# Moving the row statistics, the weight scans and some loads of a fused attention-and-GLU kernel

## The chip, the core and the metric

The kernel runs on one core of one Trainium2 chip. Time is device microseconds (us) of one execution from its first to its last instruction, with what lies around it; less is better. A profile gives the span of one execution and the times of every instruction within it. The engines are PE (matmuls), PEld (its weight loads), DVE (VectorE), ACT (ScalarE), POOL (GpSimd) and SP (SyncE, which here only issues DMAs).

## The reference

```python
x = A_x                                   # 2048 rows of 640, bf16
xn = layernorm(x)
q = xn @ wq                               # 32 heads of 192
p = softmax(q @ k_last512.T * 192**-0.5)  # each head has its own 512 keys and values
s = (p @ v_last512) @ wo
h = sigmoid(xn @ w_gate) * (xn @ w_up)    # 1536 wide
g = silu(h @ w_down)
out = x + s * g
```

## The kernel before, in words

The kernel has three stages. **Stage B** (lines 275 to 581, about the first 150 us) normalizes the rows and makes `h`. It goes over four groups `s` of 512 rows and in each over `NF` = 12 blocks `f` of 128 hidden columns (lines 474 and 479). A block is ten matmuls of 512 columns, five on the gate weights and five on the up weights (line 486), into one of four pairs of PSUM banks in turn; then ACT takes the sigmoid (line 491) and DVE multiplies into `hT_sb` (line 492). For the groups 0 to 2, `h` is stored to DRAM (`h_d`, line 554); for the last one the product with `w_down` follows at once (line 560).

**The rows of the next group** are made ready inside the blocks of this one. `load_x4` loads 512 rows in one DMA. `ln_at[s]` names the block at which the statistics begin (`ln_stats`, DVE), how many row tiles each block takes, and the block at which ACT takes the square root (`ln_rstd`). After that `ln_rest` does two row tiles in each of two blocks: `ln_apply` (DVE, line 372) writes the normalized tile `xn`, from a pool with three buffers, and SP issues a DMA transpose into `xnT` (line 441). A matmul of the next group reads all four transposed tiles. `xnT[1]` and `xnT[3]` are one buffer, `x_odd`; `xnT[0]` and `xnT[2]` lie in the big tile `mid`. In the odd groups `swap` copies halves of `x_odd` with four DMAs, and `sum_x` adds them up on DVE, for the faster matrix product of the next stage.

**Scans.** The weights are scaled by powers of two before they are added up in fp16, so an upper bound of each weight's size is wanted first. `wq` comes in 16 pieces of 480 KB into seven buffers (`scan_load`); a piece is taken by ACT (`scan_abs`, line 301: a sum of absolute values) or by DVE (`scan_fold`, lines 207 and 209: a running maximum). `abs_hw` does the same for the up weights (four pieces) and the down weights (four). The first seven `wq` pieces are loaded from SP's queue and nine from POOL's, each when the piece before it in its buffer is done. `set_scale` reduces the results, sends them through DRAM to all partitions (two POOL DMAs, lines 213 and 214), and `set_scale2` makes the scale. After that `load_raw` brings `wq` in pieces of 2 x 192 KB on 64 partitions each (POOL, line 230), and ACT and DVE scale and add them up (`scale_w`, `sum_w`). `load_k`, `scale_k` and `turn_k` load a pair of heads' keys, scale them (DVE, line 167) and transpose them with a DMA (line 172).

**Attention** (to about 680 us) has 16 runs, `r`: scores and exponentials in 16 steps `k` (`stage_s`), then eight products with the values (`stage_pv`), while `phase_s` and the loop around it issue what later runs want. **The last stage** (line 1103 on) multiplies by `wo` (steps `O`) and, for the groups 0 to 2, by `w_down` (steps `D`), with a seven-product scheme on half matrices; its extra operands are made by DVE (`scale_down`, `sum_down`). A step `D` leaves its gate rows in one of three buffers (`gate_rows`), from which POOL stores them to `gB_d` (line 1052).

Every engine and every queue takes its instructions in the order of the program; the program's order is written out by hand in the tables `sums`, `folds`, `abs_in`, `abs_at`, `ln_at` and in the conditions on `(s, f)` and `(r, k)`. An engine runs ahead of the others as far as its own waits allow, so a DMA issue that waits for nothing goes out long before the block under which it is written.

Of the kernel before, what the change touches and what calls it, by code (L numbers as in the profile page):

```python
# [8 lines left out]
AF = mybir.ActivationFunctionType  # L9
# [8 lines left out]
def kernel(  # L18
# [13 lines left out]
    nc = tc.nc  # L32
# [242 lines left out]
    with ExitStack() as bctx:  # L275
# [17 lines left out]

        wmax = bone.tile([P, NCD, NSC], BF16, name="wmax")
        mx_row = bone.tile([P, P], F32, name="mx_row")
        scans = bone.tile([P, 13], F32, name="scans")
# [6 lines left out]
        def abs_hw(n):  # L303
            v = wu_sb[:, :, 3 * n * P:3 * (n + 1) * P] if n < 4 else wd_sb[:, 3 * (n - 4):3 * (n - 3), :]
            nc.scalar.activation(
                scan_out.rearrange("p (c n) -> p c n", c=v.shape[1]), v, AF.Abs, accum_out=hw_sum[:, n:n + 1])

        def load_x(t):
            x_sb = xin_pool.tile([P, D], BF16, name=f"x_sb{t}")
            nc.sync.dma_start(x_sb[:], xf[t * P:(t + 1) * P, :])  # L310
            x_tiles[t] = x_sb[:]

        def load_x4(s):
            x_sb = xin_pool.tile([P, TQ, D], BF16, name="x_sb4")
            nc.sync.dma_start(
                x_sb[:], xf[s * 512:(s + 1) * 512, :].rearrange("(q p) d -> p q d", p=P)
            )
            for q in range(TQ):
                x_tiles[s * TQ + q] = x_sb[:, q, :]
# [131 lines left out]
        def sum_x(pi, k, x_sw):  # L451
# [12 lines left out]
            elif k == 5:  # L464
                tt(xb[HI], ev[HI], xb[HI], ALU.subtract)

        sums = {(1, 6): (0, 4), (2, 0): (0, 0), (2, 1): (0, 1), (2, 9): (0, 2), (2, 10): (0, 3), (2, 11): (0, 5),
                (3, 2): (1, 0), (3, 4): (1, 1), (3, 7): (1, 2)}
        folds = {(1, 0): 5, (1, 1): 6, (1, 9): 13, (1, 10): 14}
        abs_in = [(0, 6), (0, 7), (0, 9), (0, 10), (0, 11), (1, 1), (1, 2), (1, 4), (1, 5), (1, 7), (1, 8), (1, 10)]  # L470
        scan_act = dict(zip(abs_in, [i for i in range(NPC) if i not in folds.values()]))
        abs_at = [(2, 1), (2, 2), (2, 4), (2, 5), (2, 9), (2, 10), (3, 4), (3, 10)]
        ln_at = {0: (5, (1, 1, 2), 8), 1: (2, (1, 1, 1, 1), 6), 2: (2, (1, 1, 1, 1), 6)}
        for s in range(NST):
            hT_sb = hpool.tile([P, TQ, NF, P], BF16, name="hT_sb")
            pi = s // 2
# [2 lines left out]
            for f in range(NF):  # L479
# [31 lines left out]
                if (s, f) in folds or (s, f) in scan_act:  # L511
                    done = []
                    if (s, f) in folds:
                        done.append(folds[s, f])
                        scan_fold(wmax, done[-1], s == 1 and f == 0)
                    if (s, f) in scan_act:
                        done.append(scan_act[s, f])
                        scan_abs(done[-1], 1 + abs_in.index((s, f)))
                    for i in sorted(done):
                        if i + NSB < NPC:  # L520
                            scan_load(i + NSB, nc.gpsimd)
                if (s, f) in abs_at:
                    abs_hw(abs_at.index((s, f)))
                if s == 1 and f == NF - 1:
                    nc.vector.tensor_reduce(
                        scans[:, 0:1], wmax[:].rearrange("p c n -> p (c n)"), axis=mybir.AxisListType.X, op=ALU.max)
# [3 lines left out]
                elif s == 2 and f == 0:  # L530
                    set_scale(scans[:], mx_row)
                elif s == 2 and f == 1:
                    nc.sync.dma_start(wd_sb[:], B_w_down.rearrange("(f p) d -> p f d", p=P))
                if s == 2 and 2 <= f < 5:
                    load_raw(0, f - 2, nc.gpsimd)
                elif s == 2 and f == NF - 1:
                    set_scale2(mx_row)
                elif s == 3:
                    for c in {0: (0,), 2: (1,), 5: (2,), 8: (3,)}.get(f, ()):
                        scale_w(0, c)  # L540
                    for c in {1: (0,), 3: (1,), 6: (2,), 9: (3,)}.get(f, ()):
                        sum_w(0, c)
                        load_raw((c + 3) // NCD, (c + 3) % NCD, nc.gpsimd)
                    if f in (0, 6):
                        scale_k((0, f // 6))
                    elif f in (3, 9):
                        turn_k((0, f // 6))
                    if f == 2:
                        load_k((0, 1), nc.gpsimd)
            if s + 2 < NST:  # L550
                load_x4(s + 2)
# [203 lines left out]
    def load_wo(n):  # L755
        nc.sync.dma_start(wo_in[n % 4], wo_r[:, n * NWC:(n + 1) * NWC, :])
# [40 lines left out]
    steps = [(k[0], int(k[1:])) for k in "O0 O1 D0 D1 O2 D2 D3 O3 D4 D5 O4 O5 O6 O7".split()]  # L797
    steps += [("O", m) for m in range(8, 16)]
    wd_r = B_w_down.rearrange("(f p) d -> p f d", p=P)

    def tiles_of(j):
        kind, m = steps[j]
# [47 lines left out]
    def phase_s(r, pi, g, k, q_list, pv_list):  # L850
# [24 lines left out]
        if r in (2, 4) and k == 7:  # L875
            set_scale(*((hw_sum[:, 0:4], mx_rows[0], mx_h, 3) if r == 2 else (hw_sum[:, 4:8], mx_rows[0], mx_w, 4)))
        if r in (3, 5) and k == 0:
            set_scale2(mx_rows[0], *((mx_h, h_up, h_down, 0.25) if r == 3 else (mx_w, wd_up, wd_down)))
        if r == 6 and k == 0:
# [33 lines left out]
    for r, (pi, g) in enumerate(runs):  # L913
# [51 lines left out]
    NOD = NH * DN  # L965
    down_raw = [part(arm, n * NOD, (NH, DN), F16) for n in range(4)]
    T0, T1 = (free[n].rearrange("p a b -> p (a b)") for n in range(2))
    down_sum = [t.rearrange("p (a b) -> p a b", b=DN) for t in (T0[:, 0:NOD], T0[:, NOD:2 * NOD], T1[:, 0:NOD])]
    down_ops = [down_raw[0], down_sum[0], down_sum[1], down_raw[1], down_raw[2], down_raw[3], down_sum[2]]
# [45 lines left out]

    def keep(b, dst):
        nc.scalar.activation(dst, ps_all[:, b, 0:DN], AF.Copy)  # L1017

    def load_down(n, k, d):
        nc.sync.dma_start(down_ops[n].bitcast(BF16), wd_r[:, k * NH:(k + 1) * NH, d])  # L1020
# [84 lines left out]
    for j in range(NP):  # L1105
# [20 lines left out]
                product(j + 1, 4 - X, "A11", 0, True)  # L1126
                keep(4 - X, p1s[:])

        if j == 0:
            for part_ in (0, 0, LEFT), (4, 0, RIGHT), (5, 1, RIGHT), (3, 1, LEFT):  # L1130
                load_down(*part_)
        if j + 2 < NP:
            load_quads(j + 2)
        side(j, 0)
# [74 lines left out]
```

## Time and profile before

| | us |
|---|---|
| median of 3 runs (905.4 to 909.42) | 905.8 |
| the profiled execution | 908.94 |
| its span, from the first to the last instruction | 906.8 |
| PE busy in the span | 874.4 |
| idle PE between matmuls in stage B, groups 0 to 3 and the product with `w_down`, gaps over 0.5 us after the first 10 us | 18.45 |
| idle PE between matmuls in the last stage, gaps over 0.1 us | 4.81 |

A line of the waits names who waited, for whom, and then the total in us, the number of times and the longest. A line of the timeline has start and length in us, engine, line, operation, tiles and count; in brackets the engine's idle time before it and what ended it. A line of the table by stretches has for each engine the busy time and the count of instructions, then the clock granted to PE, the mean share of the 16 DMA engines, and GB/s. In the chain of waits a piece is start, length and who held the end.

### The profile page before, as it was taken

The numbers are of one execution on the slowest core, as the hardware profiler recorded it, in microseconds if no ns is written. First come the engines' busy times: TensorE is split into PE (matmuls) and PEld (weight loads), VectorE is DVE, ScalarE is ACT, GpSimd is POOL, SyncE is SP. The second block draws the span as 40 slices with busy tenths as digits, with TensorE's granted clock in tenths as the row PEclk, the third lists the DMA queues.
The fourth block names the chain that finished last, engine by engine and source line by source line (L and its number), as shares of the span: only waits on it lengthen the run. The fifth ranks groups of instructions, "written<-read, shape, count | busy, mean of one in ns | idle before, by whom it ended". The sixth has DMA issues, their size and how long they took to land.

```text
span 906.8 us, 18988 instructions
## 1 busy us (share of the span) xinstructions
PE 874.4 (96%) x7569; PEld 569.5 (63%) x7569; DVE 675.5 (74%) x1134; ACT 624.1 (69%) x770; POOL 235.1 (26%) x330
## 2 busy tenths in 40 slices
PE   9799798999999999999999999899998999999998
PEld 5244244576577577567667657657676776777775
DVE  4468565777687687776777777588886687888997
ACT  4687367648877968968968878664665665666662
POOL 0131124822443344245236226400000111000000
PEclk9899899999999999999999999999999999999999
DMA  9997892275999996897798799599889797466751
GB/s 269 297 265 202 177 134 88 60 170 148 214 135 206 205 227 118 210 217 116 216 228 121 203 186 145 139 261 219 198 164 247 225 300 262 147 211 220 261 178 38
DMA packets 255385, 172.90 MB, mean 191 GB/s; under 512 B 159584, under 2 KB 238688, under 8 KB 255296
## 3 DMA queue, kind: packets, MB, share of 16 engines
q1 hardware_dynamic: 246624, 144.31, 63.6%
q0 software_dynamic: 8672, 27.37, 14.6%
q8 instruction: 59, 0.97, 0.5%
q14 instruction: 30, 0.25, 0.1%
HBM read 100.47 MB, written 35.13 MB: 150 GB/s over the span
## 4 chain that ended last, share of the span: by engine, by line
PE 83%; DMA 7%; issue 3%; DVE 3%; ACT 2%; SPq 0%; POOL 0%; DVEq 0%; POOLq 0%; ACTq 0%
PE ps_all L606 20%; PE ps_all L714 19%; PE ps_all L1010 19%; PE ps_all L700 18%; PE ps_all L486 6%; DMA kraw<-in_A_k_cache_dram 3%; DMA x_odd<-xn 2%; PE ps_all L560 1%; DMA gB_d<-op 1%; DVE hT_sb L492 1%; PE ps_all L395 1%; DMA arm<-in_B_w_down_dram 1%; DMA x_sb<-in_A_x_dram 0%; ACT mid L301 0%; ACT sig_sb L491 0%
## 5 line engine op out<-in xcount | busy, mean ns | idle before, releaser
L704 ACT ACTIVATE E<-ps_all 128x1024 bf16<-128x1024 f32 x256 | 251.1, 1021 | 124.8 <-PE ps_all L700 124.2
L700 PE MATMUL ps_all<-qT,kT 64*128 64x512 bf16 x1536 | 198.1, 376 | 0.0
L714 PE MATMUL ps_all<-v_sb,E 128*128 128x193 bf16 x2048 | 175.8, 248 | 2.3 <-DVE qT L644 2.3
L714 PEld LDWEIGHTS <-E 128*128 128x128 bf16 x2048 | 171.1, 98 | 10.8 <-issue 10.6
L644 DVE TENSOR_TENSOR qT<-ps_all,qp 128x512 bf16<-128x512 f32 x174 | 115.5, 687 | 48.5 <-PE ps_all L606 38.2
L1010 PEld LDWEIGHTS <-mid 128*128 128x128 f16 x1176 | 115.0, 98 | 49.9 <-issue 5.4
L700 PEld LDWEIGHTS <-kT 64*128 64x128 bf16 x1536 | 84.9, 94 | 79.4 <-issue 4.4
L627 DVE COPY qp<-ps_all 128x512 f32<-128x512 f32 x150 | 100.5, 686 | 45.9 <-PE ps_all L606 45.9
L721 DVE TENSOR_TENSOR o_st<-ps_all,rden 128x768 bf16<-128x768 f32 x128 | 122.5, 957 | 4.6 <-DVE rden L720 0.2
L606 PE MATMUL ps_all<-mid 64*128 64x512 f16 (+1 forms) x840 | 106.4, 376 | 0.4 <-DVE qT L644 0.4
L606 PE MATMUL ps_all<-mid,arm 64*128 64x512 f16 (+1 forms) x840 | 105.6, 376 | 0.0
L606 PEld LDWEIGHTS <-mid 64*128 64x128 f16 x840 | 49.0, 94 | 44.1 <-issue 2.1
L606 PEld LDWEIGHTS <-arm 64*128 64x128 f16 x840 | 47.2, 94 | 44.7 <-issue 0.5
L1010 PE MATMUL ps_all<-arm,mid 128*128 128x320 f16 x462 | 67.5, 299 | 2.0 <-ACT p1s L1017 2.0
L830 ACT ACTIVATE mid<-mid,w_sc 128x1536 f16<-128x1536 bf16 (+1 forms) x41 | 60.2, 1493 | 0.0
L244 ACT ACTIVATE mid<-mid,w_sc 128x1536 f16<-128x1536 bf16 x37 | 58.2, 1572 | 2.7 <-DVE w_sc L222 1.7
L230 POOL DMA_DIRECT2D mid<-in_A_wq_dram x80 | 48.2, 607 | 43.9 <-DVE mid L266 43.0
L492 DVE TENSOR_TENSOR hT_sb<-ps_all,sig_sb 128x512 bf16<-128x512 f32 x48 | 32.6, 684 | 32.9 <-ACT sig_sb L491 17.0
L1010 PE MATMUL ps_all<-op,mid 128*128 128x320 f16 x378 | 55.1, 299 | 0.0
L1010 PE MATMUL ps_all<-mid 128*128 128x320 f16 x336 | 48.4, 299 | 2.8 <-DVE acc L1059 2.6
L491 ACT ACTIVATE sig_sb<-ps_all 128x512 bf16<-128x512 f32 x48 | 28.2, 594 | 31.8 <-PE ps_all L486 25.6
L486 PEld LDWEIGHTS <-wg_sb 128*128 128x128 bf16 x225 | 22.4, 101 | 43.3 <-issue 17.9
(187 smaller groups left out, 1073.0 us busy)
## 6 DMA issues: line engine op xcount, KB each, us to landing
oT_d<-oT SPq DMA_DIRECT2D x64, 384.0 KB, 5.8
mid<-oT_d SPq DMA_DIRECT2D x46, 384.0 KB, 5.3
mid<-in_A_wq_dram POOLq DMA_DIRECT2D x80, 192.0 KB, 6.4
arm<-in_A_wo_dram SPq DMA_DIRECT2D x16, 480.0 KB, 5.5
v_sb<-in_A_v_cache_dram SPq DMA_DIRECT2D x28, 192.0 KB, 5.7
kraw<-in_A_k_cache_dram SPq DMA_DIRECT2D x26, 192.0 KB, 4.5
h_d<-hT_sb SPq DMA_DIRECT2D x12, 384.0 KB, 3.8
mid<-in_A_wq_dram POOLq DMA_DIRECT2D x9, 480.0 KB, 7.5
```

What stands on the lines that cost most here:

```text
L230: eng.dma_start(raw[r], wq_r[:, c, :, g * GC:(g + 1) * GC])
L244: nc.scalar.activation(raw.bitcast(F16), raw, AF.Copy, scale=w_up)
L486: nc.tensor.matmul(gu[:, i, :], lhsT=w[:, c, f * P:(f + 1) * P], rhs=xnT[s][:, c, :], start=(c == 0), stop=(c == NCD - 1),)
L606: nc.tensor.matmul(ps_all[:, b, :], lhsT=w(r, c), rhs=x[r, c, :], start=(first and k == 0), stop=(k == len(cs) - 1), skip_group_check=True,)
L627: nc.vector.tensor_copy(dst, part(b))
L644: nc.vector.tensor_tensor(q_out(i, u, pp), part(b), t, ALU.add)
L700: nc.tensor.matmul(ps[:, b, :], lhsT=kT[h, c * PC + j, :], rhs=qT_t[r][i, j][h, pp, :], start=(j == 0), stop=(j == PC - 1),)
L704: nc.scalar.activation(E_t[r, i, pp][:, c, :, :], ps, AF.Exp, scale=scale_qk)
L714: nc.tensor.matmul(o_ps[:, q // 2, q % 2, 0:DH + 1], lhsT=E[:, c, h, q * P:(q + 1) * P], rhs=vt[:, c, 0:DH + 1], start=(c == 0), stop=(c = ...
L721: nc.vector.tensor_tensor(o_st[:, :, h * DH:(h + 1) * DH].rearrange("p (b i) d -> p b i d", b=2), o_ps[:, :, :, 0:DH], rden[:].to_broadcas ...
L830: eng.activation(t, t.bitcast(BF16), AF.Copy, scale=up)
L1010: nc.tensor.matmul(ps_all[:, b, d0:d1], lhsT=a[:, c, :], rhs=w[:, c, d0:d1], start=(start and c == 0), stop=(c == nk - 1), skip_group_chec ...
```

## The change

- `ln_at`: the statistics of the next group begin at block 2, 1 and 0 (before 5, 2, 2) and the square root is taken at block 5, 5 and 4 (before 8, 6, 6). The transposes go out at blocks 5 and 6, 6 and 7, 5 and 6 (before 8 and 9, 7 and 8, 7 and 8). `xpool` has four buffers, not three.
- `load_x4(1)` stands among the weight loads, after the fourth of six; `load_x4(s + 2)` stands at block 8, not at the end of the group.
- SP loads four scan pieces at the start, three more (4, 5, 6) at block 8 of group 0, and pieces 9 and 10 after the stores of group 0. POOL loads the other seven. ACT takes 13 pieces, DVE three (11, 12, 14).
- The up weights are scanned at blocks 3 and 4 of group 0 and 8 and 10 of group 2. The down weights are no longer scanned in stage B: in the runs 1, 3, 5 and 7 SP loads a piece of them beside `wo`, and ACT scans it in the run after; their scale is made in runs 10 and 11 (before 4 and 5).
- The six loads of the first three `raws` stand at the end of group 1, ahead of the value and key loads (before: after the first `set_scale`, in blocks 2 to 4 of group 2). `set_scale` goes from block 0 of group 2 to block 2.
- The load of `wd_sb` goes from block 1 of group 2 to block 7. In group 3, `load_k((0, 1))` goes from block 2 to 0 and its `scale_k` from 6 to 7.
- The four loads of the down operands go from the start of the last stage to run 15, step 8; the `scale_down` calls go a little later in the first step. `gate_rows` has five rows.

```diff
-        xpool = bctx.enter_context(tc.tile_pool(name="xpool", bufs=3))
+        xpool = bctx.enter_context(tc.tile_pool(name="xpool", bufs=4))
...
             if k < 2:
                 load_x(2 + k)
+            elif k == 3:
+                load_x4(1)
...
-        load_x4(1)
-        for i in range(NSB):
+        for i in range(4):
             scan_load(i, nc.sync)
...
-        folds = {(1, 0): 5, (1, 1): 6, (1, 9): 13, (1, 10): 14}
...
+        folds = {(1, 7): 11, (1, 8): 12, (1, 9): 14}
+        scan_act = {(0, 7): 0, (0, 8): 1, (0, 9): 2, (0, 10): 3, (1, 1): 4, (1, 2): 7, (1, 3): 5, (1, 5): 8, (1, 6): 6,
+                    (1, 8): 9, (1, 9): 10, (2, 0): 13, (2, 1): 15}
+        abs_at = [(0, 3), (0, 4), (2, 8), (2, 10)]
+        ln_at = {0: (2, (1, 1, 2), 5), 1: (1, (1, 1, 1, 1), 5), 2: (0, (1, 1, 1, 1), 4)}
-        ln_at = {0: (5, (1, 1, 2), 8), 1: (2, (1, 1, 1, 1), 6), 2: (2, (1, 1, 1, 1), 6)}
...
+                    if i + NSB < NPC and i not in (2, 3):
+                        scan_load(i + NSB, nc.gpsimd)
...
+                if s + 2 < NST and f == 8:
+                    load_x4(s + 2)
+                    if s == 0:
+                        for i in (4, 5, 6):
+                            scan_load(i, nc.sync)
                 if s == 1 and f == NF - 1:
+                    for c in range(3):
+                        load_raw(0, c, nc.gpsimd)
                     for hp in range(G):
                         load_v(0, hp, nc.gpsimd)
                     load_k((0, 0), nc.gpsimd)
...
-                elif s == 2 and f == 1:
+                elif s == 2 and f == 7:
                     nc.sync.dma_start(wd_sb[:], B_w_down.rearrange("(f p) d -> p f d", p=P))
-                if s == 2 and 2 <= f < 5:
-                    load_raw(0, f - 2, nc.gpsimd)
...
-                    if f == 2:
+                    if f == 0:
                         load_k((0, 1), nc.gpsimd)
...
+                if s == 0:
+                    for i in (9, 10):
+                        scan_load(i, nc.sync)
...
+            if g < 4:
+                nc.sync.dma_start(wo_in[(3 * g + 3) % 4], wd_r[:, 3 * g:3 * g + 3, :])
...
+        if r == last and k == 8:
+            for part_ in (0, 0, LEFT), (4, 0, RIGHT), (5, 1, RIGHT), (3, 1, LEFT):
+                load_down(*part_)
...
+            if pi == 0 and 1 <= g < 5 and k == 6:
+                w = wo_in[3 * g % 4]
+                nc.scalar.activation(w, w, AF.Abs, accum_out=hw_sum[:, 3 + g:4 + g])
...
+    gate_rows += [end.tile([P, D], BF16, name=f"gate{n}")[:] for n in range(2)]
...
-    for n, p in zip((0, 4, 5, 3), (1, 3, 6, 7)):
+    for n, p in zip((0, 4, 5, 3), (3, 6, 7, 8)):
         at("O0", p, scale_down, n)
```

More of the change, by code (lines that the diff above doesn't have):

```diff
@@ L295 @@
         mx_row = bone.tile([P, P], F32, name="mx_row")
-        scans = bone.tile([P, 13], F32, name="scans")
+        scans = bone.tile([P, 14], F32, name="scans")
         scan_out = bone.tile([P, 3 * D], BF16, name="scan_out")
@@ L301, in scan_abs, with abs_up @@
             nc.scalar.activation(scan_t[i], scan_t[i], AF.Abs, accum_out=scans[:, col:col + 1])
-        def abs_hw(n):
-            v = wu_sb[:, :, 3 * n * P:3 * (n + 1) * P] if n < 4 else wd_sb[:, 3 * (n - 4):3 * (n - 3), :]
+        def abs_up(n):
             nc.scalar.activation(
-                scan_out.rearrange("p (c n) -> p c n", c=v.shape[1]), v, AF.Abs, accum_out=hw_sum[:, n:n + 1])
+                scan_out.rearrange("p (c n) -> p c n", c=NCD), wu_sb[:, :, 3 * n * P:3 * (n + 1) * P], AF.Abs,
+                accum_out=hw_sum[:, n:n + 1])
         def load_x(t):
@@ L465, in sum_x @@
                 tt(xb[HI], ev[HI], xb[HI], ALU.subtract)
-        sums = {(1, 6): (0, 4), (2, 0): (0, 0), (2, 1): (0, 1), (2, 9): (0, 2), (2, 10): (0, 3), (2, 11): (0, 5),
+        sums = {(1, 5): (0, 4), (1, 10): (0, 0), (1, 11): (0, 1), (2, 7): (0, 2), (2, 8): (0, 3), (2, 9): (0, 5),
                 (3, 2): (1, 0), (3, 4): (1, 1), (3, 7): (1, 2)}
-        folds = {(1, 0): 5, (1, 1): 6, (1, 9): 13, (1, 10): 14}
-        abs_in = [(0, 6), (0, 7), (0, 9), (0, 10), (0, 11), (1, 1), (1, 2), (1, 4), (1, 5), (1, 7), (1, 8), (1, 10)]
-        scan_act = dict(zip(abs_in, [i for i in range(NPC) if i not in folds.values()]))
-        abs_at = [(2, 1), (2, 2), (2, 4), (2, 5), (2, 9), (2, 10), (3, 4), (3, 10)]
-        ln_at = {0: (5, (1, 1, 2), 8), 1: (2, (1, 1, 1, 1), 6), 2: (2, (1, 1, 1, 1), 6)}
+        folds = {(1, 7): 11, (1, 8): 12, (1, 9): 14}
[3 more added lines that the diff above has]
+        ln_at = {0: (2, (1, 1, 2), 5), 1: (1, (1, 1, 1, 1), 5), 2: (0, (1, 1, 1, 1), 4)}
         for s in range(NST):
@@ L510 @@
                     sum_x(*sums[s, f], sw)
[L511 to L521, printed above, removed]
-                if (s, f) in abs_at:
-                    abs_hw(abs_at.index((s, f)))
+                for i, fold in ((folds.get((s, f)), True), (scan_act.get((s, f)), False)):
+                    if i is None:
+                        continue
+                    if fold:
+                        scan_fold(wmax, i, i == 11)
+                    else:
+                        scan_abs(i, 1 + list(scan_act).index((s, f)))
+                    if i + NSB < NPC and i not in (2, 3):
+                        scan_load(i + NSB, nc.gpsimd)
+                if (s, f) in abs_at:
+                    abs_up(abs_at.index((s, f)))
+                if s + 2 < NST and f == 8:
[3 more added lines that the diff above has]
+                            scan_load(i, nc.sync)
                 if s == 1 and f == NF - 1:
-                    nc.vector.tensor_reduce(
-                        scans[:, 0:1], wmax[:].rearrange("p c n -> p (c n)"), axis=mybir.AxisListType.X, op=ALU.max)
+                    for c in range(3):
+                        load_raw(0, c, nc.gpsimd)
                     for hp in range(G):
@@ L530 @@
                 elif s == 2 and f == 0:
+                    nc.vector.tensor_reduce(
+                        scans[:, 0:1], wmax[:].rearrange("p c n -> p (c n)"), axis=mybir.AxisListType.X, op=ALU.max)
+                elif s == 2 and f == 2:
                     set_scale(scans[:], mx_row)
-                elif s == 2 and f == 1:
+                elif s == 2 and f == 7:
                     nc.sync.dma_start(wd_sb[:], B_w_down.rearrange("(f p) d -> p f d", p=P))
-                if s == 2 and 2 <= f < 5:
-                    load_raw(0, f - 2, nc.gpsimd)
-                elif s == 2 and f == NF - 1:
+                if s == 2 and f == NF - 1:
                     set_scale2(mx_row)
@@ L543 @@
                         load_raw((c + 3) // NCD, (c + 3) % NCD, nc.gpsimd)
-                    if f in (0, 6):
-                        scale_k((0, f // 6))
+                    if f in (0, 7):
+                        scale_k((0, f // 7))
                     elif f in (3, 9):
-                        turn_k((0, f // 6))
-                    if f == 2:
+                        turn_k((0, f // 9))
+                    if f == 0:
                         load_k((0, 1), nc.gpsimd)
-            if s + 2 < NST:
-                load_x4(s + 2)
             if s < NM3:
@@ L799, with load_down @@
     wd_r = B_w_down.rearrange("(f p) d -> p f d", p=P)
+    NOD = NH * DN
+    down_raw = dict(zip((0, 3, 4, 5), (part(arm, n * NOD, (NH, DN), F16) for n in range(4))))
+    def load_down(n, k, d):
+        nc.sync.dma_start(down_raw[n].bitcast(BF16), wd_r[:, k * NH:(k + 1) * NH, d])
     def tiles_of(j):
@@ L874, in phase_s @@
             abs_v(g, (1, 3, 4, 5).index(k))
-        if r in (2, 4) and k == 7:
+        if r in (2, 10) and k == 7:
             set_scale(*((hw_sum[:, 0:4], mx_rows[0], mx_h, 3) if r == 2 else (hw_sum[:, 4:8], mx_rows[0], mx_w, 4)))
-        if r in (3, 5) and k == 0:
+        if r in (3, 11) and k == 0:
             set_scale2(mx_rows[0], *((mx_h, h_up, h_down, 0.25) if r == 3 else (mx_w, wd_up, wd_down)))
-        if r == 6 and k == 0:
+        if r == last and k == 1:
             nc.vector.tensor_tensor(g_scale, h_down, wd_down, ALU.mult)
+        if r == last and k == 8:
+            for part_ in (0, 0, LEFT), (4, 0, RIGHT), (5, 1, RIGHT), (3, 1, LEFT):
+                load_down(*part_)
         if r == last - 3 and k == 7:
@@ L964 @@
     ops[1] = [free[2]] + [part(arm, n * NO, (KB, DN), F16) for n in range(2)] + [free[3], free[4], free[1], free[0]]
-    NOD = NH * DN
-    down_raw = [part(arm, n * NOD, (NH, DN), F16) for n in range(4)]
     T0, T1 = (free[n].rearrange("p a b -> p (a b)") for n in range(2))
     down_sum = [t.rearrange("p (a b) -> p a b", b=DN) for t in (T0[:, 0:NOD], T0[:, NOD:2 * NOD], T1[:, 0:NOD])]
-    down_ops = [down_raw[0], down_sum[0], down_sum[1], down_raw[1], down_raw[2], down_raw[3], down_sum[2]]
+    down_ops = [down_raw[0], *down_sum[:2], *(down_raw[n] for n in (3, 4, 5)), down_sum[2]]
     gate_rows = [T1[:, NOD + n * D:NOD + (n + 1) * D].bitcast(BF16) for n in range(3)]
+    gate_rows += [end.tile([P, D], BF16, name=f"gate{n}")[:] for n in range(2)]
     down_tmps = [acc[order[n]][:, d] for n in (14, 15) for d in (LEFT, RIGHT)]
@@ L1017, in keep @@
         nc.scalar.activation(dst, ps_all[:, b, 0:DN], AF.Copy)
-    def load_down(n, k, d):
-        nc.sync.dma_start(down_ops[n].bitcast(BF16), wd_r[:, k * NH:(k + 1) * NH, d])
     def scale_down(n):
@@ L1127, in ahead @@
                 keep(4 - X, p1s[:])
-        if j == 0:
-            for part_ in (0, 0, LEFT), (4, 0, RIGHT), (5, 1, RIGHT), (3, 1, LEFT):
-                load_down(*part_)
         if j + 2 < NP:
```

## The prediction, made before the changed kernel ran

> **What bounds it now.** PE is busy for 874.4 of the 906.8 us of the span, so I read the waits of PE first:
>
> ```profile
> PE ps_all L486 <- DMA x_odd<-xn: 13.2, 2, 6.7
> PE ps_all L560 <- DVE hT_sb L492: 3.0, 3, 2.0
> PE ps_all L1010 <- DVE acc L1059: 2.6, 1, 2.6
> ...
> PE ps_all L1010 <- ACT p1s L1017: 2.0, 1, 2.0
> PE ps_all L486 <- DVE hT_sb L492: 1.4, 1, 1.4
> ...
> PE ps_all L486 <- DMA mid<-xn: 0.9, 1, 0.9
> ```
>
> Half of the waiting is for `x_odd`, the transposed rows of groups 1 and 3. The timeline of PE shows the place, and a second price:
>
> ```profile
> 33.95 1.24 PE L486 MATMUL ps_all<-mid,wu_sb 128*128 128x512 bf16 x5
> 41.91 2.29 PE L486 MATMUL ps_all<-x_odd,wg_sb 128*128 128x512 bf16 x5 [6.72 <-DMA x_odd<-xn]
> 44.00 2.34 PE L486 MATMUL ps_all<-x_odd,wu_sb 128*128 128x512 bf16 x5
> 46.13 1.83 PE L486 MATMUL ps_all<-x_odd,wg_sb 128*128 128x512 bf16 x5
> 47.80 1.24 PE L486 MATMUL ps_all<-x_odd,wu_sb 128*128 128x512 bf16 x5
> ...
> 104.02 2.29 PE L486 MATMUL ps_all<-x_odd,wg_sb 128*128 128x512 bf16 x5 [6.45 <-DMA x_odd<-xn]
> ```
>
> Five matmuls take 1.08 us from start to start (33.95 against 32.87). After 6.72 us of idleness the next three fives take 5.89 us (41.91 to 47.80), not 3.24: 2.65 us for the clock, which the stretch from 40 to 45 us gives as 0.55. Group 3 pays 6.45 and 2.32 in the same way (104.02 to 109.58). With 0.87 before group 2, 1.41 in group 3 and 0.54, 0.50 and 1.96 in the product with `w_down`, stage B loses 18.45 + 4.97 = 23.4 us. In the last stage 2.61, 2.04 and 0.16 are lost, 4.8 in all. That is about what there is to win, 28 us.
>
> Why are the transposes late? Partly because they are issued late (30.82 and 91.22 us), and because the fourth waits for a buffer of `xn` until the first has landed. But the DMA engines have no room either. From the table by stretches (the last two figures are the DMA share and GB/s):
>
> ```profile
> 30.00:35.00 5.00, 5.00 (x25) 2.14 (x22) 2.02 (x5) 4.97 (x7) 0.87 (x1) 1.00 1.22 268
> 60.00:65.00 5.00, 5.00 (x25) 2.25 (x23) 3.63 (x6) 4.96 (x7) 0.10 (x1) 1.00 0.98 277
> 65.00:70.00 5.00, 5.00 (x25) 2.25 (x23) 2.86 (x6) 5.00 (x8) 0.00 (x0) 1.00 0.80 112
> 95.00:100.00 5.00, 2.57 (x12) 0.98 (x10) 0.00 (x0) 1.86 (x3) 0.00 (x0) 1.00 1.26 115
> ```
>
> From 10 to 60 us every stretch has a share of 1.01 or more, and up to 65 us none is under 0.98. So to issue earlier is not to land earlier, unless something else is pushed behind. What stands beside the transposes is in the timelines of SP and of POOL:
>
> ```profile
> 64.24 5.85 SPq L441 DMA_TRANSPOSE mid<-xn  x4
> 91.22 11.20 SPq L441 DMA_TRANSPOSE x_odd<-xn  x4
> ```
>
> ```profile
> 51.91 2.61 POOL L201 DMA_DIRECT2D mid<-in_A_wq_dram  x3 [3.03 <-DVE wmax L209]
> 54.51 2.98 POOL L181 DMA_DIRECT2D v_sb<-in_A_v_cache_dram  x4
> 89.44 3.73 POOL L230 DMA_DIRECT2D mid<-in_A_wq_dram  x6
> ```
>
> The four transposes at 64.24 land 2.6 to 3.8 us after their issue. The first three at 91.22 land 8.2 to 9.5 us after theirs: six `raws` loads had been issued at 89.44. And the value loads of line 181, written under the last block of group 1 (PE is there at about 68 us), go out at 54.51, right behind the last scan pieces: **POOL runs ahead**, as nothing holds a load into a fresh buffer.
>
> **The change, part by part.**
>
> *Group 1, won.* `load_x4(1)` goes ahead of four weight loads. The second of the six large ones landed at 14.0 us and x4, behind the sixth, took 1.8 of its own (20.4 to 22.2), so it comes at about 15.8, not 22.2. The statistics at block 2 begin behind the third product of `hT_sb` at 17.8 (0.88 + 0.21 each). ACT has two more scans before them (1.99 each, from the rows of line 305: 1.80 + 0.19) and two table loads (1.28 each), all beside PE. I get the square root at 24.1 and the transposes issued from 25.1 to 28.9; four scan pieces, not seven, are ahead of them on SP's queue (the fourth landed at 28.3). With about 5 us, as at 30.82 beside POOL's pieces, the last lands at 33 to 34; PE wants it at 33.95 + 1.08 = 35.03. So 6.72 + 2.65 = 9.4 us go. If ACT or a piece is late by 2 us, 1 us of it stays.
>
> *Group 2, lost.* Group 1 now ends 25.9 us after its start (12 x 2.16), at 60.9. Until then the DMA engines have the same bytes to move as before: x, weights, 16 pieces, the stores of `h`, the swap, x4(2). All of that had landed at 62.3 us before, with the share full; nothing in the change makes it less. The four transposes need 0.77 each (two landed so far apart, 68.05 and 68.83), so with nothing else they are done at 62.3 + 3.1 = 65.4. But POOL issues its last piece, 13, behind the scan of piece 6 at block 6, about 55 us, and then without a wait six `raws`, four values and two keys. The transposes are issued at 54 to 58 and stand behind the swap on SP's queue. At least these 12 loads cost their own time: `raws` land 0.8 apart when alone (issues 0.6 apart at 136.9 and 147.2), values 0.7, keys 0.5 to 1.7: 4.8 + 2.8 + 1.6 = 9.2, done at 74.6. At the price of 91.22, (9.4 - 2.6) / 6 = 1.13 for each load beside a transpose, they cost 13.6, done at 79.0. I take the middle, **77**. PE is then idle from 60.9 to 77 and pays the clock: 16.1 + 2.65, where before it paid 0.87.
>
> The Trainium skill speaks against this part too: "DMA: Bandwidth & Descriptors", section "Issuing engines are not separate DMA queues", says that DMAs of all issuing engines run on the same 16 DMA engines. By that the twelve loads cost at least their own time: rows at 74.6, which would make the result 895.3. The rows at 91.22 agree, and show more.
>
> *Group 3, won.* `raws` are gone from the transposes, which are issued in blocks 5 and 6 of group 2, some 12 us before they are wanted; the 13.0 us load of `wd_sb` is issued after them, behind the last on the same queue. `set_scale`, whose first DMA took 9.9 us beside `wd_sb`, has the queue free. 6.45 + 2.32 go; if `wd_sb` still overtakes, up to that much stays.
>
> *End of stage B.* The chain of waits has "116.03 15.62 DMA kraw": the keys' load stood beside the first transpose of keys (17.8 us to landing, 5.0 for the second alone), `scale_k` waited on DVE, and behind it the products of `hT_sb`, for which PE waited 4.41. Now that load goes out at block 0, before the transposes; two scans of ACT (2 x 1.99) are gone as well. `raws` still stand beside the transpose. I leave 1.2 of the 4.41 (between 0 and all).
>
> *Attention.* Four `wd` pieces of 480 KB: 1.5 us each on the queue in odd runs, where the keys' transpose landed at 287.4 and PE wanted it at 294. Four scans of 1.99 us on ACT in the product phase, after which ACT sat idle 5.25 us (before 262.07). Both are covered; uncovered they cost 4 x 2 = 8. Moving `set_scale` to runs 10 and 11 costs DVE what it cost in runs 4 and 5.
>
> *Last stage.* DVE waited 5.9 us for a down operand (issued at 686.64), so PE waited 2.61; now it is issued some 18 us sooner, in run 15, where four loads of about 1.5 us push back SP's transposes of the last outputs, which only the steps from `O8` on read. ACT waited 2.8 us for a store of a gate row (759.19 to 765.06), so PE waited 2.04 and 0.16; the two further rows end that. 4.6 of 4.8 go; nothing goes at worst, and a late `scale_down` (0.72) can cost as much.
>
> **The sum.** Idle in stage B before 23.4; after 16.1 + 2.65 + 1.2 = 19.9; won 3.5, and 4.6 in the last stage: 8.1 us. The durations are those of an execution of 908.94 (span 906.8), 3.1 over the median; I take the difference from the median: 905.8 - 8.1 = **897.7**.
>
> **Rivals.**
>
> *Transposes get an even share (888).* With each of the two queues served in turn by equal work, the four transposes need 2 x 3.1 behind the swap, which I put at 60.9, and land at 67. PE idles 6.1, pays 2.65 and 1.2: 13.4 won, with 4.6 it is 18 us. If POOL's loads do not touch them at all (65.4 or sooner, no clock), it is 23 to 26, 880. For it: at 30.82 two transposes landed at 36.3 and 36.9 with POOL's pieces in flight. Against: the three at 91.22 landed only as the last of six loads did (100.6 to 102.6 against 101.5). The Trainium skill, "DMA: Bandwidth & Descriptors", section "Queues, rings and completion order", says that each DMA engine serves its queues in turn, a packet at a time, with about 9 to 17 descriptors in one; by that it would be this case, and the rows at 91.22 don't agree.
>
> *Slower: the loads stall as beside the keys' transpose (924).* There a transpose landed 17.8 us after its issue, not 5.0, with four loads beside it: 3.2 for each. Twelve at that price put group 2's rows at 65.4 + 38 = 104; 27 us more idle than I forecast, 19 over the median: 924. It decides from 85 us on, 1.64 for each load; over 0.5% slower is 89.6. For it: the same kinds of loads. Against: the transposes of rows at 91.22 paid a third of it, and those of 64.24 next to nothing beside values and keys.
>
> *It doesn't do what it says (905).* The wait moves whole from groups 1 and 3 to group 2 (rows at 81 to 90), or the last stage keeps its 4.8 behind another operand: within 4.5 us.
>
> **Chances.** Forecast (893 to 901) 0.48; even share or better 0.21; no change 0.15; slower 0.16. Half a per cent, 4.5 us, is about what a measurement of this kernel can tell from no change. Faster by more 0.69, within 0.15, slower 0.16. The range goes from 880, the best of the even share, to 912: the forecast with group 2's rows at 79 (2 us), the attention's 8 uncovered and nothing won in the last stage (4.6). I put some 0.04 below it and 0.14 above.
>
> **What would show it.** Right: PE's wait for `x_odd` before group 1 is gone, and one wait for `mid<-xn` of 12 to 18 us stands before group 2, with transposes landing as the last POOL loads do; none before group 3; the two of line 1010 gone. Wrong: POOL's `raws` issued only after 65 us, or transposes that land beside them within 5 us, or scan pieces so late that ACT holds up the sigmoids in group 1.

## The result

The changed kernel takes **914.7 us** (median of 20 runs, 907.2 to 921.4), the kernel before it 905.0 (20 runs beside them, 898.7 to 916.7): a ratio of **1.011, 95% interval 1.008 to 1.013**. It is slower by about 10 us, where 8 us less were forecast, and it lies outside the range. Its profiled execution was the quickest of the 20: 907.24 us, span 905.5. In the next set of runs it took 910.0, the kernel before it 904.2 (ratio 1.007, 1.004 to 1.010).

The waits of PE in the kernel after (who waited for whom; total, times, longest):

```profile
PE ps_all L487 <- DMA mid<-xn: 21.7, 1, 21.7
PE ps_all L720 <- DVE qT L650: 7.1, 2, 5.8
```

The waits for `x_odd` and those of the last stage are gone, as forecast. Two others hold the loss: the rows of group 2, and `qT` (the queries) in the attention, for which PE waited 2.3 us once before. The timeline of PE at group 2:

```profile
82.50 2.29 PE L487 MATMUL ps_all<-mid,wg_sb 128*128 128x512 bf16 x5 [21.72 <-DMA mid<-xn]
84.58 1.76 PE L487 MATMUL ps_all<-mid,wu_sb 128*128 128x512 bf16 x5
86.18 1.24 PE L487 MATMUL ps_all<-mid,wg_sb 128*128 128x512 bf16 x5
```

PE stands still for 21.7 us, and the first two fives then take 3.68 us (82.50 to 86.18) instead of 2.16: 1.5 more for the clock. The queues of SP and of POOL, and the table by stretches (DMA share and GB/s last), show what happened meanwhile:

```profile
53.80 18.27 SPq L442 DMA_TRANSPOSE mid<-xn  x4
```

```profile
55.64 3.85 POOL L230 DMA_DIRECT2D mid<-in_A_wq_dram  x6
```

```profile
65.00:70.00 5.00, 0.00 (x0) 0.00 (x0) 0.95 (x1) 0.00 (x0) 0.77 (x1) 0.51 0.97 188
...
75.00:80.00 5.00, 0.00 (x0) 0.00 (x0) 0.00 (x0) 0.00 (x0) 0.00 (x0) 0.50 1.31 95
```

POOL did run ahead, and its six `raws` went out at 55.64 beside the transposes of 53.80. The values and keys did not follow at once, though: the first value load went out at 65.63, the other three from 71.02 on and the keys at 73.24. SP issued its four transposes at 53.8, 55.1, 61.0 and 68.9, where 54 to 58 was forecast; the rows themselves were normalized by 56.4. The share rises from 0.97 to 1.31 while the bytes fall from 188 to 95 GB/s: **a full share doesn't mean that much is moved**. The rows landed at 74.5, 76.3, 80.7 and 82.25 us; forecast was 77 for the last.

The second loss is in the chain of waits (start, length, what held the end) and in the stretches around it:

```profile
506.56 10.62 DMA kraw<-in_A_k_cache_dram
...
519.55 10.50 PE ps_all L720 x107
```

```profile
510.00:512.50 2.50, 2.50 (x24) 1.22 (x21) 1.15 (x2) 2.06 (x4) 0.00 (x0) 1.00 1.08 17
512.50:515.00 2.50, 1.29 (x16) 1.14 (x14) 0.00 (x0) 2.47 (x3) 0.00 (x0) 1.00 0.40 34
```

A key load of run 10 takes 10.6 us; behind it DVE scales the keys, then makes `qT`, and PE waits 5.76 us for that. From 510 to 515 the DMA engines move 17 and 34 GB/s with a share of 1.08 and 0.40. The DMAs issued from 503 to 508 us (count, size, us from issue to landing) name a neighbour:

```profile
kraw<-in_A_k_cache_dram SPq DMA_DIRECT2D x2, 192.0 KB, 10.7
mx_d<-w_sc POOLq DMA_DIRECT2D x1, 0.5 KB, 11.1
```

`mx_d` is the first DMA of `set_scale`: 128 values of 4 bytes written to DRAM. This one belongs to the scale of the down weights, the second `set_scale` of the attention (the first stands in run 2), which the change had moved to run 10. It went out at 504.89 us, 1.0 ahead of the first key load (505.87).

**Theories.** T1: the transposes of group 2 and POOL's loads slow each other, and taking the loads away brings the rows early. T2: the store of 4-byte values holds up the DMA engines for some microseconds; where it catches a key load, PE pays. Rivals: the bytes of group 2 are owed in any case and only move the wait; run 10's wait comes from the `w_down` pieces and scans that the change put into the runs.

### The profile page after: what moved, and what is told of

Its sections match the earlier page's. It is cut to its first block, busy times and chain, and to the rows that moved or that the text cites. A ratio compares the mean times of both kernels' runs of the same rounds, so it can differ in the third digit from the quotient of the medians.

```text
span 905.5 us, 18985 instructions
## 1 busy us (share of the span) xinstructions
PE 869.6 (96%) x7569; PEld 568.7 (63%) x7569; DVE 674.3 (74%) x1132; ACT 625.9 (69%) x772; POOL 232.4 (26%) x328
## 3 DMA queue, kind: packets, MB, share of 16 engines
q1 hardware_dynamic: 249536, 147.26, 65.6%
## 4 chain that ended last, share of the span: by engine, by line
PE 81%; DMA 5%; ACT 2%; DVE 2%; SPq 1%; issue 1%; DVEq 0%; ACTq 0%
PE ps_all L1028 23%; PE ps_all L720 19%; PE ps_all L612 18%; PE ps_all L706 17%; PE ps_all L487 3%; DMA kraw<-in_A_k_cache_dram 2%; DMA mid<-xn 1%; PE ps_all L566 1%; DMA x_sw<-x_odd 1%; ACT E L710 1%; SPq L740 1%; ACT arm L765 0%; ACT mid L244 0%; SPq L442 0%; DVE arm L1012 0%
## 5 line engine op out<-in xcount | busy, mean ns | idle before, releaser
L1028 PE MATMUL ps_all<-op,mid 128*128 128x320 f16 x378 | 55.1, 299 | 0.0
```

The source lines that it names most:

```text
L1028: nc.tensor.matmul(ps_all[:, b, d0:d1], lhsT=a[:, c, :], rhs=w[:, c, d0:d1], start=(start and c == 0), stop=(c == nk - 1), skip_group_chec ...
```

## Experiments on group 2

**The changed kernel once more.**

> The changed kernel as it is, for a second profile. The first one ran 907.2 us where the median of 20 is 914.7, so it had some 7 us less of waiting than most. Theory (POOL's loads hold group 2's transposes): PE's wait before group 2 is 21 to 30 us, and the time 910 to 918; what is above the first profile lies in that wait. Rival (the difference to most runs lies in the attention): that wait is 21 to 22 again and the waits of line 720 have grown beyond 7.1 us.

910.0 us; PE waits 23.5 us for group 2, 6.7 in run 10: 1.8 and 0.9 more than in the first profile, so neither account of the expectation alone. This is the base of the next two and of the first experiment on the store, run on the same chip.

**`raws` behind the scale.**

```diff
-                    for c in range(3):
-                        load_raw(0, c, nc.gpsimd)
...
                 elif s == 2 and f == 2:
                     set_scale(scans[:], mx_row)
+                    for c in range(3):
+                        load_raw(0, c, nc.gpsimd)
```

> The changed kernel, but the six loads of the first raws stand behind the first set_scale in group 2, so that POOL can't issue them early; values and keys still go out beside group 2's transposes. Theory (POOL's loads beside the transposes are what holds them): the transposes land some 8 to 12 us sooner, at 71 to 74 us, PE's wait before group 2 is 10 to 14, and the time falls by about as much, to some 903 to 907. Rival (SP's own queue holds them: four stores of h, two scan pieces and the swap stand ahead): the wait stays at 20 us or more and the time at 912 to 917.

911.1 us, ratio 1.007 (1.004 to 1.010): nothing won, where 903 to 907 was expected. The waits of PE, in an execution of 919.4, 8 us over the median:

```profile
PE ps_all L487 <- DMA mid<-xn: 14.7, 1, 14.7
PE ps_all L487 <- DMA x_odd<-xn: 7.6, 1, 7.6
```

Group 2 waits 14.7 us and not 23.5, but the six loads now go out at 95.06, beside the transposes of group 3 (92.40), and PE waits 7.6 us for those: the collision moved with them. Run 10's wait was 6.4 us.

**All twelve loads behind the scale.**

```diff
-                    for c in range(3):
-                        load_raw(0, c, nc.gpsimd)
-                    for hp in range(G):
-                        load_v(0, hp, nc.gpsimd)
-                    load_k((0, 0), nc.gpsimd)
+                    pass
...
                 elif s == 2 and f == 2:
                     set_scale(scans[:], mx_row)
+                    load_k((0, 0), nc.gpsimd)
+                    for c in range(3):
+                        load_raw(0, c, nc.gpsimd)
+                    for hp in range(G):
+                        load_v(0, hp, nc.gpsimd)
```

> The changed kernel with all of POOL's raws, value and key loads behind the first set_scale in group 2. Theory: only scan pieces stand beside group 2's transposes; they land at 64 to 67 us, the wait is 3 to 7, the clock keeps its pace or loses one short window, and the time is 893 to 900. If the loads then come too late for group 3 (keys and raws are wanted at its first block), a wait of up to 5 us of DVE shows there. Rival (SP's own queue): the wait stays at 15 us or more, the time over 908.

909.6 us, ratio 1.005 (1.002 to 1.007); 893 to 900 was expected. PE waits 10.3 us before group 2, 6.8 at groups 1 and 3, 6.0 in run 10. Of POOL's work two scan pieces alone still stood beside the transposes, which took 12.5 us to land instead of 20.2 (median, below). So the twelve loads cost group 2 some 13 us (23.5 against 10.3), but neither of the two later places on POOL's queue won time.

**The same loads on SP's queue, behind the transposes**, and two scan pieces with them (their scans and the `set_scale` of group 2 go a few blocks later). SP issues in the order of the program, so these loads go out only after the transposes: in this run those were issued from 53.63 to 63.3 us, and the first of the loads at 64.01.

```diff
-                    (1, 8): 9, (1, 9): 10, (2, 0): 13, (2, 1): 15}
+                    (1, 8): 9, (1, 9): 10, (2, 3): 13, (2, 4): 15}
...
-                    if i + NSB < NPC and i not in (2, 3):
+                    if i + NSB < NPC and i not in (2, 3, 6, 8):
...
                         for i in (4, 5, 6):
                             scan_load(i, nc.sync)
+                    else:
+                        for i in (13, 15):
+                            scan_load(i, nc.sync)
...
-                        load_raw(0, c, nc.gpsimd)
+                        load_raw(0, c, nc.sync)
                     for hp in range(G):
-                        load_v(0, hp, nc.gpsimd)
-                    load_k((0, 0), nc.gpsimd)
+                        load_v(0, hp, nc.sync)
+                    load_k((0, 0), nc.sync)
...
-                elif s == 2 and f == 2:
+                elif s == 2 and f == 5:
                     set_scale(scans[:], mx_row)
```

> Changed kernel with GpSimd's loads of group 2 put on SP's queue behind the transposes, and nothing else (the second set_scale stays in runs 10 and 11). Theory (the two costs are apart): PE waits 3 to 7 us before group 2 and 4 to 7 us in run 10; 898 to 903 us, the difference to the version with both being the 8 us of the late store. Rival (the wait in run 10 came of the shift in time that group 2 gave): no wait in run 10, 890 to 895 us.

895.6 us, ratio **0.992 (0.989 to 0.994)**. It ran on another chip, so the ratios to the kernel before are what can be compared: 1.5% under the changed kernel's 1.007, some 14 us. PE waits:

```profile
PE ps_all L723 <- DVE qT L653: 6.6, 1, 6.6
PE ps_all L487 <- DMA mid<-xn: 4.3, 1, 4.3
```

4.3 us before group 2, and run 10's wait stands as it was: the two costs are apart. The time came out 2 us under the range I had expected; on this chip the kernel before took 902.0, 2 less than beside the base.

## Experiments on the scale's store

**The second `set_scale` at the start of runs 9 and 10.**

```diff
-        if r in (2, 10) and k == 7:
+        if (r, k) in ((2, 7), (9, 0)):
...
-        if r in (3, 11) and k == 0:
+        if r in (3, 10) and k == 0:
```

> The changed kernel, but the down weights' set_scale is moved from run 10, step 7, to run 9, step 0, and its second half from run 11 to run 10. Theory (the first DMA of set_scale, 128 values of 4 bytes to DRAM, stalls the DMA engines for some 8 us, and in run 10 the key load of that run is caught in it): PE's wait of 5.8 us in run 10 goes, and 4 to 8 us of the time with it. Rival (the wait in run 10 comes from the four pieces of down weights or from the shifted start, not from that store): it stays within 2 us of 5.8, and the time within 3 us of the changed kernel's.

902.0 us, ratio 0.997 (0.995 to 0.999), 8 us under the changed kernel beside it. In the profile (an execution of 896.6, the quickest) both of PE's waits on line 720 are gone from the attention, with 0.4 us left at its start, and PE waits 19.7 us for group 2.

**The kernel before with that one move of the change**: `set_scale` and `set_scale2` from runs 4 and 5 to 10 and 11, nothing else.

```diff
-        if r in (2, 4) and k == 7:
+        if r in (2, 10) and k == 7:
...
-        if r in (3, 5) and k == 0:
+        if r in (3, 11) and k == 0:
...
-        if r == 6 and k == 0:
+        if r == 12 and k == 0:
```

> Kernel before with the second set_scale alone moved from runs 4 and 5 to runs 10 and 11 (and the product g_scale from run 6 to 12). Theory (its store catches the key load of run 10, as in the changed kernel): a wait of PE of 3 to 6 us in run 10 and a half clock behind it; 908 to 913 us, 4 to 8 over the kernel before. Rival (the wait in run 10 comes from the w_down pieces or from the scans that the change put into the runs): within 2 us of the kernel before.

913.9 us, ratio **1.010 (1.007 to 1.014)**: 9 us lost, as much as the whole change loses. Of PE's waits:

```profile
PE ps_all L714 <- DVE qT L644: 5.8, 1, 5.8
```

The pieces of `w_down` and their scans are not in this kernel, so that rival falls. The half clock behind the wait lasted 6.8 us, which is 3.4 us of lost work: 5.8 + 3.4 = 9.2. In exchange the wait of 2.3 us that the profile of the kernel before has in run 12 is not here, and the two profiled executions differ by 4.8 us only; the profile of the kernel before with the new last stage alone (below), whose attention is the same, doesn't have that wait either.

**The changed kernel without the store.** Run 10's `set_scale` reads the row that run 2's wrote, so the maximum of `w_down` is left out.

```diff
-    def set_scale(wm, mx_row, mx=mx, n=0):
+    def set_scale(wm, mx_row, mx=mx, n=0, store=True):
...
-        nc.gpsimd.dma_start(mx_d[n][:].rearrange("o p -> p o"), mx)
+        if store:
+            nc.gpsimd.dma_start(mx_d[n][:].rearrange("o p -> p o"), mx)
...
-            set_scale(*((hw_sum[:, 0:4], mx_rows[0], mx_h, 3) if r == 2 else (hw_sum[:, 4:8], mx_rows[0], mx_w, 4)))
+            set_scale(*((hw_sum[:, 0:4], mx_rows[0], mx_h, 3) if r == 2 else (hw_sum[:, 4:8], mx_rows[0], mx_w, 3, False)))
```

> Changed kernel, but the second set_scale (runs 10 and 11) leaves out its store of 128 values of 4 bytes and reads the row of the first set_scale instead: the maximum of w_down is left out of the result. Everything else stands where it stood. Theory (this store holds up all DMA for some 7 us): key loads of run 10 land within 6 us of their issue, PE's wait of 5.8 us in run 10 is gone; 901 to 905 us. Rival (DVE's and GpSimd's order in run 10, or the row's read, is what costs): key loads land 9 us or later, the wait stays at 5 to 7 us; 908 to 912 us.

904.5 us, ratio 0.999 (0.996 to 1.002). Key loads from 503 to 520 us:

```profile
kraw<-in_A_k_cache_dram SPq DMA_DIRECT2D x4, 192.0 KB, 4.1
```

The wait of run 10 is gone with the store, and PE waits 25.8 us for group 2. In this execution the keys also went out later than before (513 against 506 us), behind SP's other work, so this run alone doesn't tell the stall from that shift; the next two show the stall by itself.

**Four stores of other shapes**, added to the best kernel (below), at the start of runs 5 to 8; nobody reads them.

```diff
+    probe_d = dram.tile([4, P, P], F32, name="probe_d")
...
+        if k == 0 and 5 <= r < 9:
+            n, eng = {5: (1, nc.gpsimd), 6: (16, nc.gpsimd), 7: (1, nc.sync), 8: (P, nc.gpsimd)}[r]
+            eng.dma_start(probe_d[r - 5].rearrange("a b -> (a b)")[0:P * n].rearrange("(p n) -> p n", n=n), mx_rows[0][:, 0:n])
```

> The fastest kernel so far (second set_scale at the start of runs 9 and 10, GpSimd's loads of group 2 on SP's queue), with four stores added to DRAM rows that nobody reads, 128 partitions each, from one tile: at the start of run 5 4 bytes of each partition from GpSimd, run 6 64 bytes from GpSimd, run 7 4 bytes from SP, run 8 512 bytes from GpSimd. Theory (rows of 4 bytes hold up the DMA engines): the stores of runs 5 and 7 land 7 to 12 us after issue, with a stretch of 3 us or more in which hardly a packet of another queue moves, those of 6 and 8 within 6 us without one. Rival A (GpSimd's queue does it): run 7's lands within 5 us, the other three late. Rival B (128 small rows of any size below 512 bytes): run 6's is late too. The time is 893 to 905 us, the more the later the key loads come.

The stores of run 5 (4 bytes), 6 (64 bytes) and 7 (4 bytes, from SP), each with its size in all and us to landing, and a stretch behind run 5's issue at 313.1 us:

```profile
probe_d<-mx_all POOLq DMA_DIRECT2D x1, 0.5 KB, 12.5
...
probe_d<-mx_all POOLq DMA_DIRECT2D x1, 8.0 KB, 5.1
...
probe_d<-mx_all SPq DMA_DIRECT2D x1, 0.5 KB, 9.6
```

```profile
320.00:322.50 2.50, 2.50 (x26) 1.29 (x24) 2.06 (x5) 1.21 (x3) 0.00 (x0) 1.00 0.93 5
```

The 4-byte stores take 12.5 and 9.6 us, from either queue; rows of 64 and of 512 bytes take 5.1 and 4.9. For 2.5 us 5 GB/s move with a share of 0.93, and for the next 2.5 us 16 GB/s. Rival A (POOL's queue does it) and rival B (any small row does it) fall. The kernel took 890.4 us (ratio 0.983, 0.979 to 0.988, of four runs), no more than without the stores: here no load that was wanted soon stood in the way, and the stall cost nothing that can be seen.

**Where the 4 bytes lie.** Run 5: 4 bytes each 512 bytes apart; run 6: 32 bytes each side by side; run 7: 4 bytes 64 bytes apart; run 8: 4 bytes side by side; all from POOL.

The new buffer is as above.

```diff
+        if k == 0 and 5 <= r < 9:
+            n, step = {5: (1, P), 6: (8, 8), 7: (1, 16), 8: (1, 1)}[r]
+            rows = probe_d[r - 5].rearrange("a b -> (a b)")[0:P * step].rearrange("(p n) -> p n", n=step)
+            nc.gpsimd.dma_start(rows[:, 0:n], mx_rows[0][:, 0:n])
```

> The fastest kernel so far, with four stores of GpSimd added to DRAM rows that nobody reads, 128 partitions each: at the start of run 5 4 bytes of each partition 512 bytes apart, run 6 32 bytes of each side by side, run 7 4 bytes 64 bytes apart, run 8 4 bytes side by side. Theory (many partitions' values in one stretch of 512 bytes is what holds up the DMA engines): run 8's store lands 9 us or more after its issue, with some microseconds in which hardly a packet moves; run 5's within 6 us, runs 6 and 7 within 7. Rival (a row of 4 bytes is what does it, wherever it lies): runs 5, 7 and 8 all land after 9 us or more, run 6 within 6. The time is 888 to 900 us by both, as the stores' places in runs 5 and 7 cost little before.

```profile
probe_d<-mx_all POOLq DMA_DIRECT2D x1, 0.5 KB, 5.7
...
probe_d<-mx_all POOLq DMA_DIRECT2D x1, 0.5 KB, 6.7
...
probe_d<-mx_all POOLq DMA_DIRECT2D x1, 0.5 KB, 12.6
```

These are runs 5, 7 and 8; run 6's took 5.1 us. In run 5 values side by side had taken 12.5 us and those 512 bytes apart take 5.7; in run 8 rows of 512 bytes had taken 4.9 and values side by side take 12.6. Only the 4-byte values side by side stall. The Trainium skill, "DMA: Bandwidth & Descriptors", section "Specifications", says that transfers below 512 bytes make the DMA engine read, modify and write; here 4 bytes alone took 5.7 and 6.7 us, so by these runs it is not the row's size alone but that many such rows lie close together. Where between 4 and 64 bytes apart the stall ends, and what makes it, was not tried. Run 8's store caught that run's keys (issued 6.0 us behind it, landed 12.1 after that), and PE waited 6.0 us there: 897.7 us, where the same kernel without it took 893.1; both were timed against the kernel before (0.992, 0.988 to 0.995, against 0.985, 0.980 to 0.989).

**One more move of a scale**, the first one of the attention from run 2, block 7, to block 0, in the best kernel.

```diff
-        if (r, k) in ((2, 7), (9, 0)):
+        if (r, k) in ((2, 0), (9, 0)):
```

> The fastest kernel so far, with the first set_scale of the attention moved too, from run 2, block 7, to its block 0. Theory (its store catches run 2's key load or DVE's turn of the queries, and PE waits 1.8 us in run 2): that wait goes; 1 to 3 us under it, 889 to 893 us. Rival (the wait of run 2 is of DVE's own order): within 1 us of it, 892 to 895.

A miss: 893.3 us, ratio 0.990 (0.987 to 0.994), and PE's wait in run 2 grew from 1.8 to 6.3 us.

```profile
kraw<-in_A_k_cache_dram SPq DMA_DIRECT2D x2, 192.0 KB, 12.8
...
mx_d<-w_sc POOLq DMA_DIRECT2D x1, 0.5 KB, 13.5
```

The store went out at 221.3 us and the keys at 225.7 and 226.7, 4.4 us behind it, into the stall. In the best kernel the store went out at 226.92, 1.3 and 0.4 us behind the two key loads: the first landed after 4.8 us, and DVE waited for the second until 235.8, which is PE's wait of 1.8 us there. So loads issued up to 6 us behind the store were caught, and those issued up to 1 us ahead of it were caught in some runs and not in others (below). The table of that better kernel shows the stall at its barest (share and GB/s last):

```profile
232.00:234.00 2.00, 2.00 (x21) 1.00 (x17) 1.51 (x3) 1.56 (x3) 0.00 (x0) 1.00 0.00 0
```

## Experiments on the rest, and the best kernel

**The change to the last stage alone**, in the kernel before.

```diff
+    def load_down(n, k, d):
+        nc.sync.dma_start(down_raw[n].bitcast(BF16), wd_r[:, k * NH:(k + 1) * NH, d])
...
+        if r == last and k == 8:
+            for part_ in (0, 0, LEFT), (4, 0, RIGHT), (5, 1, RIGHT), (3, 1, LEFT):
+                load_down(*part_)
...
+    gate_rows += [end.tile([P, D], BF16, name=f"gate{n}")[:] for n in range(2)]
...
-    for n, p in zip((0, 4, 5, 3), (1, 3, 6, 7)):
+    for n, p in zip((0, 4, 5, 3), (3, 6, 7, 8)):
...
-        if j == 0:
-            for part_ in (0, 0, LEFT), (4, 0, RIGHT), (5, 1, RIGHT), (3, 1, LEFT):
-                load_down(*part_)
```

> Kernel before with the last part of the change alone: the four down operands loaded in run 15, block 8, scaled at positions 3, 6, 7 and 8 of O0, and five gate rows. Theory (both waits of line 1010 go, nothing takes their place): 4 to 5 us under the kernel before. Rival (the early loads push back other work, or other operands are late next): within 2 us of the kernel before.

899.4 us, ratio **0.995 (0.992 to 0.997)**: 5 us won. PE waits for nothing in the last stage any more.

**Both cures**: the changed kernel with the loads on SP's queue and the second `set_scale` at the start of runs 9 and 10.

> Changed kernel with the second set_scale at the start of runs 9 and 10, and with all that GpSimd loads beside group 2's transposes put on SP's queue behind them: scan pieces 13 and 15 and the loads of raws, values and keys (the scans of 13 and 15 move from blocks 0 and 1 to 3 and 4 of group 2, set_scale from block 2 to 5). Theory (transposes and GpSimd's loads slow each other, 256-byte against 4608-byte packets): group 2's rows land at 65 to 68 us, PE waits 4 to 7 us for them and at most 2 for the clock, nothing before group 3; 885 to 890 us. Rival (the bytes are owed anyway and only come later): rows at 70 to 72, or a wait of 4 us or more before group 3 or for the late scale; 894 to 900 us.

**893.1 us, ratio 0.985 (0.980 to 0.989)**; it beats both kernels. That is 2.2% under the changed kernel, 20 us, where the two cures alone gave 8 and 14; its median lies over the 885 to 890 I expected, in which two of its six runs are (885.1 and 885.8). In the execution of 885.1 PE waits 2.9 us before group 2 and the clock stays at 1.00:

```profile
PE ps_all L487 <- DMA mid<-xn: 2.9, 1, 2.9
```

```profile
60.00:65.00 5.00, 2.07 (x11) 0.77 (x10) 4.93 (x7) 0.76 (x2) 0.00 (x0) 1.00 0.94 186
```

The transposes issued from 50 to 75 us, in the changed kernel and then in this one (count, us to landing):

```profile
mid<-xn SPq DMA_TRANSPOSE x4, 20.2
```

```profile
mid<-xn SPq DMA_TRANSPOSE x4, 5.8
```

The transposes land 5.8 us after their issue instead of 20.2 (medians), and in the same answers the six `raws` 7.7 instead of 15.3: **both are quicker one behind the other than side by side**, so the rival that the bytes are owed in any case falls.

## Why the prediction was wrong

- **Group 1, won: right.** The transposes went out at 24.20 (25.1 forecast), the last landed at 34.0 (33 to 34), and PE doesn't wait.
- **Group 2, lost: right in kind, too small.** The step that failed is the price of the twelve loads, "I take the middle, 77". It was 82.25: PE lost 21.7 + 1.5 where 16.1 + 2.65 stood, 4.5 more. The upper price, 79.0 from the row of 91.22, was passed too: there six loads met the transposes, here two scan pieces stood in the way as well (they landed at 65.3 and 70.7). The lower one, 74.6, let nothing slow anything, and I had given it half the weight. Nor did POOL issue all twelve "without a wait": only the six `raws` had gone out before 65.6, and the keys left at 73.24. What I had not priced at all is that SP's issues stretch beside them: the fourth transpose went out at 68.9 and not at 58.
- **Group 3, won, and the end of stage B: right.** No wait before group 3; 1.1 us is left in the product with `w_down` where I had put 1.2.
- **Attention: wrong, and the largest miss.** The step that failed is "Moving `set_scale` to runs 10 and 11 costs DVE what it cost in runs 4 and 5". It priced DVE and not the DMA. In run 10 the store caught the keys: 5.8 us and the clock, 8 to 9 us by the two experiments that moved it. What differs is the place. In the kernel before, run 4's store went out at 308.6, 1.2 and 0.4 us behind that run's two key loads, which landed after 4.8 and 4.6 us; in run 10 the keys came 1.0 us behind it and took 10.7. Being ahead is no guarantee: key loads issued 0.9 us ahead of a store landed after 9.8 us in run 12 of the kernel before and after 13.3 in run 10 of the same kernel with the scale moved there, but after 3.8 in run 12 of the same kernel with the new last stage. What decides is not shown. A row of before had shown the cost: PE had waited 2.3 us for `qT` in run 12, with these DMAs issued from 568 to 572 us:

```profile
kraw<-in_A_k_cache_dram SPq DMA_DIRECT2D x2, 192.0 KB, 9.3
...
mx_d<-w_sc POOLq DMA_DIRECT2D x1, 0.5 KB, 9.0
```

- I had read the 9.9 us of the first `set_scale` as the company of `wd_sb`. Every one of these stores in all 14 traces takes 7 to 14 us, whatever is beside it.
- **Last stage: right.** Forecast 4.6, measured 5 us.
- **The sum.** On the two profiled executions: -8.1 forecast, + 4.5 for group 2, + 4.8 for the attention (2.3 of waiting and 1.7 of clock before, 7.1 and 1.7 after, half of 3.4 us at half clock) gives +1.2; the two differ by -1.7, and their spans by -1.3. By stage: the attention begins at 150.4 in both, so stage B won nothing instead of 3.5; the last stage begins at 684.6 and not 680.3, 4.3 later; and it takes 5.6 us less, 1.0 more than forecast. The medians differ by +9.7. The one profiled execution of the changed kernel was the quickest of 20, while that of the kernel before lay 4 us over its median; the second one profiled took 910.0, with 1.8 us more before group 2 and 0.9 more in run 10. What the rest, 4.7 us up to 914.7, consists of no trace here shows.
- **The rivals.** Not the even share: beside POOL's pieces and loads the transposes got far less. The loads did not reach the 85 us from which the slower case was to decide; rows at 81 to 90 were the case of "no change", and that one came true for group 2. What made the kernel slower was in none of the cases. I had bounded the attention by ACT and the queue (8 us in all), not by a stall.

## What to carry to other kernels

When a step is moved, look at each DMA it issues, however small, for its time from issue to landing, and at which loads that are wanted soon go out in the microseconds behind it. A second queue was no help here, where the DMA engines were full: what could wait did better on the same queue, behind what couldn't. Read GB/s beside the share: a share of 1 with 17 GB/s is a stall, not work.

## What the runs showed of the hardware

128 values of 4 bytes written side by side to DRAM took 7 to 14 us to land in every trace. In the five stalls followed here all DMA together moved less than 60 GB/s for some 5 to 8 us of that, and nothing at all from 232 to 236 us of the best kernel; spread 64 bytes apart the values took 6.7, in rows of 32 bytes 5.1. Four DMA transposes took 5.3 us (median to landing, group 1 of the changed kernel) and 5.8 (group 2 of the best), 12.5 beside two scan pieces of POOL, 20.2 beside those and the loads behind them. The clock granted to PE fell to half for 3.4 us or a multiple (6.8, 10.2, up to 27.3) after every wait of 4 us and more. Waits of 2 to 3.1 us fell on both sides: half clock after 2.3 (run 12 of the kernel before), 2.5 and 2.9 (group 2 of the kernel with the first scale moved to block 0, and of the one with the spread stores) and 3.1 (last stage of the kernel before with the scale moved), none after 2.6 (last stage of the kernel before), 2.9 and 3.0 (group 2 of the best kernel, and of the one with the first four stores). The Trainium skill, "TensorE: Matmul & The Clock Gate", section "Part 1: The HAM clock gate (the "warmup" mystery)", gives a window of about 3.4 us, which agrees, and an idle one as the condition for half speed, with which a wait of 2.3 us doesn't agree.
